# Agent attention with two feed-forward layers on one core: q blocks among k, two v blocks a step, combined weights inside the last q steps

## Chip, cores and metric

One core of a Trainium2 chip. The metric is the device time of one execution in microseconds (us); lower is better.

## What is computed

```python
scale = 1.0 / np.sqrt(q.shape[-1])
def sm(a, b):
    s = scale * (a @ b.transpose(0, 2, 1))
    s = s - s.max(-1, keepdims=True)
    e = np.exp(s)
    return e / (e.sum(-1, keepdims=True) + 1e-09)
agent_v = sm(agents, k) @ v          # 49 agents, k and v: 12480 x 128
x = sm(q, agents) @ agent_v          # q: 12480 x 128
h = x @ w_in                         # 128 x 2048
x = (h * (1.0 / (1.0 + np.exp(-h)))) @ w_out
h = x @ w2_in
out = (h * np.cos(h)) @ w2_out
```

q, k, v and agents are fp32. The four weight matrices come as 64-bit floats, 128 x 2048 or 2048 x 128.

## The kernel before

Precision is kept by splitting: a number is held as a high and a low part in the fp32r type, and a product is three matmuls (high x high, low x high, high x low). Each of the 16 weight pieces (512 columns of 64-bit words) is taken apart by `split_a` and `split_b`: an absolute value on ACT (L260), five DVE operations on the words (L264, L265, L269, L272, L275), a cast on ACT for the high part (L285), two POOL operations for the low part (L286, L287).

The 12480 rows of q, k and v are cut into 13 blocks (12 of 1024 rows and one of 192). The work goes through three stages.

1. **k pass.** For each k block, `T` turns the raw rows on PE (L323: eight 128 x 128 transposes into `h`) and ACT copies them to SBUF (`xT`, L327). `k_scores` multiplies by the agents (L357), ACT keeps the scores (`sT`, L360) and DVE takes a running maximum (`kmax`, L361). Ten weight pieces are split in the same steps.
2. **q steps.** Step i turns q block i, computes the scores of q block i-1 (`q_scores`, L337) and their exponentials (`q_exp`: maximum L117, subtraction L120, Exp L121), normalises block i-2 (`q_norm`: sum L128, + 1e-9 L130, reciprocal L132, product on POOL L133), splits block i-3 (`q_split`: L145 to L147, tile `pk`) and turns block i-4 in two halves (`p_out`: transposes L156 into the PSUM bank `y2`, copy to `pT` L161). The maximum over all k is made by `k_max_b` and `k_max_c` (result `mk`, L380). A list `at` says in which step a k block gets its exponential (`k_exp`, L383); its turn (`k_turn`, L394, copy `eT` L396) and its product with v (`av`, L408, summed in the bank `pav`) follow one and two steps later. In nearly all steps that is one k, v block.
3. **End of the attention.** `pav` is brought together (`halves`, L472, L475), normalised (`ag`, L479) and spread (`pn`, L481). The first product of layer 1 is not made with x: the agents' values are multiplied into `w_in` first, so that layer 1 takes the 49 probabilities `pT` and combined weights. This is `av_times_w` (L550 to L552, with the high and low parts `avh`, `avl` of the agents' values), `apart` (`hr` L557, four subtractions into `w3` L560) and `in_place` (L564, L565, L568 write `w2l`, `w2h`). It stands behind the attention, in the part whose order is written out by hand.

Then follow 25 blocks of up to 512 tokens through both layers. `L1_rest` (L590) and `L1_h` (L602) make h, `L1_act` the Silu (L610), `L1_y` (L634, L635, L638) the output; layer 2 follows five groups (`LAG`) behind. The in-place pair of the last quarter of the combined weights stands in group 1 of this loop.

What sets the order: up to the end of the attention the framework's scheduler orders the instructions of each engine by dependencies and by the order in the code; the splitting of weights has a lower priority (`LATER`). Every engine takes its instructions in order, and so does the SP queue, which issues all loads. The list `todo` sets the order of q, k and v loads: all k, then q and v in turn, with `NRAW` (7) buffers for q and k, `NV` (3) for v and 3 for weight pieces (`wraw`). From the combined weights on, the order is the one written in the code.

Of the kernel before, what the change touches and what calls it, by code (L numbers as in the profile page):

```python
# [22 lines left out]
NRAW = 7  # L23
NV = 3
# [4 lines left out]
LAG = 5  # L29
LINE = 32  # L30
# [3 lines left out]
def agent_attention_moe_moe_kernel(ctx, tc, q, k, v, agents, w_in, w_out, w2_in, w2_out, out):  # L34
# [79 lines left out]
    def q_exp(S, ps, between):  # L114
# [26 lines left out]
    def q_split(S):  # L141
        _, p, n = blocks[S]
        e = es.pop(S)
# [24 lines left out]
    def p_out_two(S):  # L168
        pp = bank2()
        for g in range(2):  # L170
            p_turn(S, g, pp[:, g, :])
        for g in range(2):
            p_keep(S, g, pp[:, g, :], nc.scalar.copy)

    with ExitStack() as att:
# [3 lines left out]
        eT_p = att.enter_context(tc.tile_pool(name="eT", bufs=2))  # L179
# [11 lines left out]

        ag = one_p.tile([NA, C], F32, name="ag")
# [678 lines left out]
```

## Time and profile before

| | |
|---|---|
| median of 3 runs | 1120.99 us (1120.79 to 1121.43) |
| profiled execution | 1122.09 us |
| its span | 1120.3 us |
| PE busy | 1085.3 us, 97% |
| DVE busy | 979.1 us, 87% |
| ACT busy | 923.9 us, 82% |
| POOL busy | 541.4 us, 48% |

The span is what the profiler recorded from the first to the last instruction of the profiled execution; its own time is 1.8 us longer. PE is one array with two rows in the views: PE for matmuls, PEld for weight loads. A busy share over the whole span says little here, since the long loop over both layers makes up most of it. The stages ahead of the loop are read by stretches and by timelines.

### The profile page before, as it was taken

What the parts mean: (1) busy time and instruction counts of PE and PEld (TensorE: products, weight loads), DVE (VectorE), ACT (ScalarE), POOL (GpSimd) and SP (SyncE); (2) the same over time, 40 slices, a digit from 0 to 9 for tenths busy, and PEclk for the clock granted to TensorE, in tenths of its full rate; (3) what the DMA queues carried; (4) which work ended last, traced back from release to release, by engine and by line L of the source; (5) the groups of instructions that cost most, each with busy time, mean ns of one, the idle gap of its engine ahead of it and who ended that gap; (6) DMA issues with size and microseconds to landing.
All of it is one profiled execution on the core that took longest, in us unless ns stands there. A gap on an engine that the chain in (4) does not pass through costs nothing.

```text
span 1120.3 us, 14139 instructions
## 1 busy us (share of the span) xinstructions
PE 1085.3 (97%) x5227; PEld 850.5 (76%) x5227; DVE 979.1 (87%) x1053; ACT 923.9 (82%) x1006; POOL 541.4 (48%) x278
## 2 busy tenths in 40 slices
PE   8878899999999999999999999999999999999997
PEld 4667666777777777777777777777777777788996
DVE  5898369999999999999999999999999999999997
ACT  6757588888888888888888888888888888888876
POOL 2578303444455544445554444555444455555455
PEclk9889889999999999999999999999999999999999
DMA  8655100000000000000000000000000000000000
GB/s 321 228 207 192 53 6 6 1 16 16 10 6 16 16 1 16 16 10 6 16 15 1 16 16 11 6 16 15 1 16 16 11 6 14 14 1 14 10 8 16
DMA packets 66221, 38.68 MB, mean 35 GB/s; under 512 B 52523, under 2 KB 57184, under 8 KB 66152
## 3 DMA queue, kind: packets, MB, share of 16 engines
q1 hardware_dynamic: 66152, 37.78, 11.3%
q8 instruction: 41, 0.67, 0.3%
q14 instruction: 28, 0.23, 0.1%
HBM read 27.58 MB, written 6.39 MB: 30 GB/s over the span
## 4 chain that ended last, share of the span: by engine, by line
PE 82%; ACT 2%; DVE 1%; issue 1%; POOL 1%; POOLq 0%; ACTq 0%; DVEq 0%
PE y L634 15%; PE y L638 15%; PE y L635 15%; PE h L602 9%; PE h L676 8%; PE h L678 8%; PE h L677 8%; PE h L590 4%; ACT g L610 1%; POOL g2l L735 1%; DVE g L717 1%; ACT n L690 0%; ACT g1h L617 0%; DVE n L700 0%; DVE g2h L726 0%
## 5 line engine op out<-in xcount | busy, mean ns | idle before, releaser
L735 POOL TENSOR_TENSOR g2l<-g,g2h 128x1024 fp32r<-128x1024 f32 (+2 forms) x200 | 465.5, 2349 | 512.6 <-DVE g1l L625 502.8
L700 DVE SCALAR_TENSOR_TENSOR n<-n,h 128x1024 f32<-128x1024 int32 (+3 forms) x202 | 239.1, 1185 | 65.2 <-ACT n L690 52.0
L690 ACT ACTIVATE n<-h,quarter 128x1024 int32<-128x1024 f32 (+3 forms) x202 | 219.8, 1089 | 89.3 <-PE h L678 89.3
L625 DVE TENSOR_TENSOR g1l<-g,g1h 128x1024 fp32r<-128x1024 f32 (+2 forms) x200 | 239.7, 1198 | 16.8 <-ACT g1h L617 9.6
L717 DVE TENSOR_TENSOR g<-n,h 128x1024 f32<-128x1024 f32 (+3 forms) x202 | 238.0, 1179 | 3.3 <-ACT n L709 0.2
L610 ACT ACTIVATE g<-h 128x1024 f32<-128x1024 f32 (+2 forms) x200 | 199.6, 998 | 36.4 <-PE h L602 36.3
L709 ACT ACTIVATE n<-n,halfpi 128x1024 f32<-128x1024 f32 (+3 forms) x202 | 225.6, 1119 | 0.8 <-DVE n L700 0.8
L617 ACT CAST g1h<-g 128x1024 fp32r<-128x1024 f32 (+2 forms) x200 | 204.8, 1024 | 3.3
L726 DVE CAST g2h<-g 128x1024 fp32r<-128x1024 f32 (+2 forms) x196 | 154.3, 788 | 7.5
L634 PE MATMUL y<-g1h,o1h 128*128 128x512 f32 (+2 forms) x400 | 156.7, 392 | 0.6 <-DVE x2l L663 0.5
L634 PE MATMUL y<-g2h,o2h 128*128 128x512 f32 (+2 forms) x400 | 154.5, 386 | 1.1 <-DVE o L757 0.9
L676 PE MATMUL h<-x2h,i2h 128*128 128x512 f32 (+2 forms) x400 | 154.1, 385 | 1.0 <-DVE g L717 1.0
L635 PE MATMUL y<-g2h,o2l 128*128 128x512 f32 (+2 forms) x400 | 154.4, 386 | 0.0
L635 PE MATMUL y<-g1h,o1l 128*128 128x512 f32 (+2 forms) x400 | 154.2, 386 | 0.0
L678 PE MATMUL h<-x2l,i2h 128*128 128x512 f32 (+2 forms) x400 | 153.7, 384 | 0.0
L677 PE MATMUL h<-x2h,i2l 128*128 128x512 f32 (+2 forms) x400 | 153.7, 384 | 0.0
L602 PE MATMUL h<-pT,w2h 128*128 128x512 f32 (+2 forms) x400 | 132.9, 414 | 0.0
L638 PE MATMUL y<-g2l,o2h 128*128 128x512 f32 (+2 forms) x400 | 122.2, 386 | 1.9 <-POOL g2l L735 1.9
L638 PE MATMUL y<-g1l,o1h 128*128 128x512 f32 (+2 forms) x400 | 121.6, 385 | 0.0
L634 PEld LDWEIGHTS y<-g1h,o1h 128*128 128x128 f32 x400 | 75.3, 188 | 22.0 <-DVE x2l L663 8.5
L602 PEld LDWEIGHTS h<-pT,w2h 128*128 128x128 f32 x400 | 67.6, 189 | 31.0 <-issue 24.0
L638 PEld LDWEIGHTS y<-g2l,o2h 128*128 128x128 f32 x400 | 74.8, 188 | 17.7 <-POOL g2l L735 3.1
(131 smaller groups left out, 1183.8 us busy)
## 6 DMA issues: line engine op xcount, KB each, us to landing
raw<-in_q_dram SPq DMA_DIRECT2D x12, 512.0 KB
vraw<-in_v_dram SPq DMA_DIRECT2D x12, 512.0 KB
raw<-in_k_dram SPq DMA_DIRECT2D x11, 512.0 KB
out_dram<-o SPq DMA_DIRECT2D x88, 64.0 KB
wraw<-in_moe_w_in_dram SPq DMA_DIRECT2D x8, 512.0 KB
wraw<-in_moe_w_out_dram SPq DMA_DIRECT2D x8, 512.0 KB
x<-pT SPq DMA_DIRECT2D x88, 38.0 KB
raw<-in_k_dram SPq DMA_DIRECT2D x2, 256.0 KB
```

The lines of the kernel that those rows point to most:

```text
L602: nc.tensor.matmul(out=h1s[g, k][:, j, :toks(t)], lhsT=w2h[:, 128 * c:128 * c + 128], rhs=x, start=False, stop=True)
L625: i = v.tensor_tensor(out=gl, in0=f, in1=b32(gh), op=ALU.subtract)
L634: nc.tensor.matmul(out=y, lhsT=wh[:, c, :], rhs=gh[:, j, :], start=(c == 0), stop=False)
L635: nc.tensor.matmul(out=y, lhsT=wl[:, c, :], rhs=gh[:, j, :], start=False, stop=False)
L638: nc.tensor.matmul(out=y, lhsT=wh[:, c, :], rhs=gl[:, j, :], start=False, stop=(c == NCH - 1))
L676: nc.tensor.matmul(out=y, lhsT=i2h[:, c, :], rhs=xh, start=True, stop=False)
L677: nc.tensor.matmul(out=y, lhsT=i2l[:, c, :], rhs=xh, start=False, stop=False)
L678: nc.tensor.matmul(out=y, lhsT=i2h[:, c, :], rhs=xl, start=False, stop=True)
L700: v.scalar_tensor_tensor(out=b32(n)[:, p], in0=n[:, p], scalar=-2.0 * PI, in1=h2s[g, k][:, p], op0=ALU.mult, op1=ALU.add)
L709: sc.activation(out=r[:, p], in_=r[:, p], func=AF.Sin, bias=halfpi)
L717: v.tensor_tensor(out=f[:, p], in0=r[:, p], in1=h[:, p], op=ALU.mult)
L735: i = (v if (g, k) == (NG - 1, 1) else gp).tensor_tensor(out=gl[:, p], in0=f[:, p], in1=b32(gh)[:, p], op=ALU.subtract)
```

## The change

- **Order.** Three q steps (`EARLY_Q`) run inside the k pass, behind k blocks 4, 7 and 10, without weight splitting; six pieces (`EARLY_W`) are split there instead of ten. Behind the k pass a loop goes on with the q steps and takes two k, v blocks in each (`at[S] = 1 + S // 2`): exponentials in step b, turn and product in step b + 1.
- **Loads.** `todo` follows that order. Buffers: raw 5 instead of 7, v 4 instead of 3, `eT` 3 instead of 2.
- **Combined weights.** `avh`, `avl` and `combine` now stand inside the two q steps behind the last v product, in the part that the scheduler orders, two pairs of column blocks through the bank `h2`; the last q steps follow. Nothing of it is left in the loop of layer 1.
- **The 1e-9** of a q block's sum is a 50th column of three fixed tiles `three_e`, so the addition L130 goes.
- The small Silu that loads its table has no other input than `ones`; the scheduler now puts it at the start of ACT.

```text
lines of the changed kernel: turn L325, xT L329, q scores L339, k scores L359,
sT L362, k exponential L385, k turn L396, eT L398, av L410, pn L489,
combined weights L497 to L499, hr L504, w3 L507, in place L513 to L515,
L1_rest L612, L1_h L624, Silu L632
```

```diff
-NRAW = 7
-NV = 3
+NRAW = 5
+NV = 4
 NWARM = 9
 LATER = 150
 WIDE = 512
 LAST = (416, 416, 384)
 LAG = 5
+EARLY_Q = (4, 7, 10)
+EARLY_W = (2, 4, 6, 8, 10, 12)
...
-        e = e_p.tile([128, 8, NA], F32, tag="e", name="e")[:p, :n]
+        es[S] = three_e[S % 3][:p, :n]
+        e = es[S][:, :, 0:NA]
...
         z = e_p.tile([128, 8], F32, tag="z", name="z")[:p, :n]
-        nc.vector.tensor_reduce(out=z, in_=e, op=ALU.add, axis=AX.X)
-        run(between, 1)
-        nc.vector.tensor_scalar(out=z, in0=z, scalar1=1e-9, scalar2=None, op0=ALU.add)
+        nc.vector.tensor_reduce(out=z, in_=es[S], op=ALU.add, axis=AX.X)
...
-        eT_p = att.enter_context(tc.tile_pool(name="eT", bufs=2))
+        eT_p = att.enter_context(tc.tile_pool(name="eT", bufs=3))
         xT_p = att.enter_context(tc.tile_pool(name="xT", bufs=2))
...
+        three_e = [one_p.tile([128, 8, NA + 1], F32, name=f"e{j}") for j in range(3)]
...
-        todo = [(k, "k", S) for S in range(NS)]
-        for S in range(NS + 2):
-            todo += [(q, "q", S)] if S < NS else []
-            todo += [(v, "v", S - 2)] if S >= 2 else []
+        at = [1 + S // 2 for S in range(NS)]
+        todo, t = [], 0
+        for S in range(NS):
+            todo.append((k, "k", S))
+            if S in EARLY_Q:
+                todo.append((q, "q", t))
+                t += 1
+        for b in range(NS):
+            todo += [(q, "q", t + b)] if t + b < NS else []
+            todo += [(v, "v", S) for S in range(NS) if at[S] == b]
...
+        def q_step(t):
+
+            if t < NS:
+                T("q", t)
+            if 4 <= t < NS + 4:
+                p_out(t - 4, 0)
+            split_b()
+            load_piece()
+            work = split_a() if t >= len(EARLY_Q) else []
+            if 2 <= t < NS + 2:
+                q_norm(t - 2, work)
+            if 3 <= t < NS + 3:
+                q_split(t - 3)
+            run(work, 1)
+            if 1 <= t < NS + 1:
+                q_scores(t - 1)
+                q_exp(t - 1, pss.pop(("q", t - 1)), work)
+            run(work, 6)
+
+        def q_step_end(t):
+            if 4 <= t < NS + 4 and groups(t - 4) == 2:
+                p_out(t - 4, 1)
+
         for _ in range(2):
             load_piece()
-        work = []
+        t = 0
         for i in range(NS + 1):
-            T(*(("k", i) if i < NS else ("q", 0)))
+            if i < NS:
+                T("k", i)
             if i >= 1:
                 k_scores(i - 1)
-            if i >= 2 and i % 6 != 5:
+            if i in EARLY_Q:
+                q_step(t)
+                t += 1
+            if i in EARLY_W:
                 split_b()
-                work = split_a()
-                run(work, 6)
+                run(split_a(), 6)
                 load_piece()
 
-        at = [2, 3, 4, 5, 6, 6, 7, 8, 9, 10, 10, 11, 12]
-        for i in range(1, NS + 2):
-            if i < NS:
-                T("q", i)
-            if i == 2:
+        k_max_b()
+        early = t
+        while t < early + 3 or raws or todo:
+            b = t - early
+            for S in range(NS):
+                if at[S] == b - 1:
+                    k_turn(S)
+            q_step(t)
+            if b == 0:
                 k_max_c()
-            if i >= 4:
-                p_out(i - 4, 0)
             for S in range(NS):
-                if at[S] == i:
+                if at[S] == b:
                     k_exp(S)
-                if at[S] == i - 1:
-                    k_turn(S)
-            split_b()
-            load_piece()
-            work = split_a()
-            if i >= 2:
-                q_norm(i - 2, work)
-            if i >= 3:
-                q_split(i - 3)
-            run(work, 1)
-            if i <= NS:
-                q_scores(i - 1)
-                q_exp(i - 1, pss.pop(("q", i - 1)), work)
-            run(work, 6)
-            if i == 1:
-                k_max_b()
-            for S in range(NS):
-                if at[S] == i - 2:
+                if at[S] == b - 1:
                     av(S)
-            if i >= 4:
-                p_out(i - 4, 1)
-        while half_split or loaded or to_load:
-            split_b()
-            load_piece()
-            run(split_a(), 6)
-
-        halves = xT_p.tile([128, 2, 512], F32, tag="xT", name="halves")[:, 0, :C + 1]
+            q_step_end(t)
+            t += 1
+
...
-        p_out_two(NS - 2)
-        end = banky("y2")
-        p_turn(NS - 1, 0, end)
+        avh, avl = (eT_p.tile([128, 512], F32R, tag="eT", name=nm)[:, :256] for nm in ("avh", "avl"))
+        nc.vector.tensor_copy(out=avh, in_=pn)
+        nc.vector.tensor_tensor(out=avl, in0=pn, in1=b32(avh), op=ALU.subtract)
+
...
+        def combine(j, cast):
+            pair = bank2()
+            for x in range(2):
+                av_times_w(pair[:, x, :], j + x, True)
+            apart(pair, j, cast)
+            pair = bank2()
+            for x in range(2):
+                av_times_w(pair[:, x, :], j + x, False)
+            in_place(pair.rearrange("p x d -> p (x d)"), slice(512 * j, 512 * j + 1024))
+
+        for j, cast in ((0, nc.vector.tensor_copy), (2, nc.scalar.copy)):
+            q_step(t)
+            combine(j, cast)
+            q_step_end(t)
+            t += 1
+        while t < NS + 4:
+            q_step(t)
+            q_step_end(t)
+            t += 1
+        assert not (half_split or loaded or to_load or es)
...
-        b01, a01, b23 = pair_bank(), pair_bank(), pair_bank()
-        a2, a3 = banky("y1"), banky("y2")
...
-            if g == 1:
-                in_place(a3, q3)
-                in_place_low(a3, q3)
```

How the instructions move. In the names, `h` with a number is a PSUM tile of scores or turned rows, `y` with a number a bank of turned probabilities, `raw` and `vraw` loaded rows.

PE in a middle step, from one q score block to the next. Before:

```order
L408 MATMUL y_173<-vraw,eT 49x128 x5
L156 MATMUL y_867<-ident,pk 128x128 x4
L408 MATMUL y_173<-vraw,eT 49x128
L394 MATMUL h_891<-ident,sT 128x128 x4
L323 MATMUL h_794<-ident,raw 128x128 x8
L156 MATMUL y_884<-ident,pk 128x128 x4
L408 MATMUL y_173<-vraw,eT 49x128 x7
L156 MATMUL y_947<-ident,pk 128x128 x4
L337 MATMUL h_919<-agT,xT 128x98 x8
```

After:

```order
L156 MATMUL y_880<-ident,pk 128x128 x4
L396 MATMUL h_886<-ident,sT 128x128 x4
L396 MATMUL h_893<-ident,sT 128x128 x4
L156 MATMUL y_911<-ident,pk 128x128 x4
L339 MATMUL h_937<-agT,xT 128x98 x5
L325 MATMUL h_900<-ident,raw 128x128 x8
L339 MATMUL h_937<-agT,xT 128x98 x3
L410 MATMUL y_175<-vraw,eT 49x128 x16
```

One v block's eight products stood in pieces between the other work; now sixteen products of two blocks follow each other, and two k turns stand between two halves of probabilities.

ACT at the end of the attention, up to the first Silu of layer 1. Before:

```order
L161 CAST pT<-y_1441 128x512
L145 CAST pk<-e 96x2x49
L161 CAST pT<-h_1464 128x512 x2
L161 CAST pT<-y_1476 128x192
L545 ACT_TABLE_LOAD
L545 ACTIVATE silu<-ones 128x1
L564 ACTIVATE w2l<-h,from_67 32x1024
L565 CAST w2h<-h 96x1024
L557 CAST hr<-h 128x1024
L564 ACTIVATE w2l<-y_1541,from_67 32x512
L565 CAST w2h<-y_1541 96x512
L610 ACTIVATE g_1593<-h 128x1024
```

After:

```order
L513 ACTIVATE w2l<-h_1430,from_67 32x1024
L514 CAST w2h<-h_1430 96x1024
L161 CAST pT<-y_1446 128x512
L504 CAST hr<-h_1461 128x1024
L513 ACTIVATE w2l<-h_1474,from_67 32x1024
L514 CAST w2h<-h_1474 96x1024
L161 CAST pT<-y_1484 128x512
L145 CAST pk<-e_121 96x2x49
L161 CAST pT<-y_1490 128x512
L161 CAST pT<-y_1501 128x512
L632 ACT_TABLE_LOAD
L632 ACTIVATE g_1573<-h 128x1024
```

The in-place writes move ahead of the last probability copies, and the table load now stands directly in front of the first Silu instead of ahead of the combined weights.

PE in the k pass, from the turn of k block 5. Before:

```order
L323 MATMUL h_272<-ident,raw 128x128 x8
L357 MATMUL h_285<-xT,agk 64x512 x2
L323 MATMUL h_304<-ident,raw 128x128 x8
L357 MATMUL h_317<-xT,agk 64x512 x2
L323 MATMUL h_323<-ident,raw 128x128 x8
L357 MATMUL h_336<-xT,agk 64x512 x2
L323 MATMUL h_355<-ident,raw 128x128 x8
```

After, from the turn of q block 0:

```order
L325 MATMUL h_278<-ident,raw 128x128 x8
L325 MATMUL h_307<-ident,raw 128x128 x8
L359 MATMUL h_320<-xT,agk 64x512 x2
L325 MATMUL h_326<-ident,raw 128x128 x8
L359 MATMUL h_339<-xT,agk 64x512 x2
L325 MATMUL h_358<-ident,raw 128x128 x8
L359 MATMUL h_371<-xT,agk 64x512 x2
L325 MATMUL h_377<-ident,raw 128x128 x8
L339 MATMUL h_395<-agT,xT 128x98 x8
L325 MATMUL h_408<-ident,raw 128x128 x8
```

Turns of q blocks 0 and 1 and the scores of q block 0 stand among the k blocks; q block 0's scores come behind the turn of q block 1, eight rows after its own turn.

## Rows read from the trace of the kernel before

**Rows 1.** Busy time by stretches (us; PE, PEld, DVE, ACT, POOL, clock, DMA, GB/s).
```profile
0.00:37.00 37.00, 31.51 (x174) 16.22 (x175) 24.02 (x54) 25.46 (x37) 8.80 (x13) 1.00 0.81 301
37.00:121.00 84.00, 68.51 (x544) 59.83 (x543) 70.66 (x118) 56.87 (x110) 61.78 (x57) 0.88 0.57 197
121.00:138.00 17.00, 13.16 (x90) 9.20 (x88) 5.91 (x18) 6.25 (x14) 5.29 (x10) 0.74 0.06 23
```

**Rows 2.** Timeline, 20 to 46 us (start, us, engine, line, operation).
```profile
24.73 1.08 PE L357 MATMUL h<-xT,agk 128*64 128x512 f32 x4 [1.67 <-ACT xT L327]
...
43.76 0.16 DVE L380 TENSOR_SCALAR mk<-y 128x1 f32<-128x1 f32 x1 [0.88 <-PE y L379]
```

**Rows 3.** Timeline of PE, 45 to 61 us.
```profile
46.92 3.70 PE L337 MATMUL h<-agT,xT 128*128 128x98 f32 x16 [0.84 <-DVE z L130]
...
51.36 1.09 PE L323 MATMUL h<-ident,raw 128*128 128x128 f32 x8
52.29 0.60 PE L156 MATMUL y<-ident,pk 128*128 128x128 f32 x4
52.82 0.86 PE L408 MATMUL y<-vraw,eT 128*49 128x128 f32 x12
...
58.86 2.03 PE L337 MATMUL h<-agT,xT 128*128 128x98 f32 x16
```

**Rows 4.** Groups of DVE by line, 0 to 148 us (busy us, mean ns).
```profile
L269 DVE SCALAR_TENSOR_TENSOR a<-wraw,a 128x512 uint32<-128x512 uint32 x16 | 17.8, 1110 | 0.2
L265 DVE TENSOR_SCALAR a<-m 128x512 uint32<-128x512 uint32 x16 | 14.5, 909 | 0.2
L275 DVE SCALAR_TENSOR_TENSOR r<-wraw,m 128x512 f32<-128x512 uint32 x16 | 14.0, 874 | 0.2
L272 DVE TENSOR_SCALAR m<-a 128x512 uint32<-128x512 uint32 x16 | 10.2, 640 | 0.1
L264 DVE TENSOR_SCALAR m<-m 128x512 f32<-128x512 f32 x16 | 9.3, 581 | 1.8 <-ACT m L260 1.8
...
L117 DVE TENSOR_REDUCE m<-h 128x8 f32<-128x392 f32 (+1 forms) x13 | 6.9, 534 | 9.5 <-PE h L337 9.5
```

**Rows 5.** Line 130 alone (duration ns: min, median, max).
```profile
L130 DVE TENSOR_SCALAR z<-z x13: 157/330/1246, 46.7 to 125.4; 128x8 f32<-128x8 f32 x12, 96x2 f32<-96x2 f32 x1
```

**Rows 6.** Timeline of all engines, 128 to 149 us.
```profile
128.92 0.51 PE L408 MATMUL y<-vraw,eT 96*49 96x128 f32 x2 [3.00 <-DMA vraw<-in_v_dram]
...
136.25 0.43 DVE L542 TENSOR_TENSOR avl<-h,avh 128x256 fp32r<-128x256 f32 x1
...
138.18 0.80 PE L550 MATMUL h<-w2h,avh 128*128 128x512 f32 x1 [0.84 <-ACT pT L161]
...
138.37 1.28 ACT L545 ACT_TABLE_LOAD   x1
...
139.66 0.20 ACT L545 ACTIVATE silu<-ones 128x1 f32<-128x1 f32 x1
...
141.20 1.22 DVE L557 CAST hr<-h 128x1024 fp32r<-128x1024 f32 x1 [4.52 <-PE h L552]
...
142.46 1.72 DVE L560 TENSOR_TENSOR w<-h,hr 32x256 fp32r<-32x256 f32 x4
...
143.37 1.11 ACT L564 ACTIVATE w2l<-h,from 32x1024 fp32r<-32x1024 f32 x1 [3.51 <-issue]
...
144.50 1.01 ACT L565 CAST w2h<-h 96x1024 fp32r<-96x1024 f32 x1
...
145.54 1.23 DVE L568 TENSOR_TENSOR w2h<-h,w2l 32x1024 fp32r<-32x1024 f32 x1 [1.36 <-ACT w2h L565]
...
148.03 1.02 ACT L610 ACTIVATE g<-h 128x1024 f32<-128x1024 f32 x1 [0.31 <-PE h L602]
```

**Rows 7.** Timeline of ACT, 154 to 158 us: two Silus of layer 1.
```profile
154.04 1.02 ACT L610 ACTIVATE g<-h 128x1024 f32<-128x1024 f32 x1
...
157.35 1.02 ACT L610 ACTIVATE g<-h 128x1024 f32<-128x1024 f32 x1
```

More of the change, by code (lines that the diff above doesn't have):

```diff
@@ L142, in q_split @@
         _, p, n = blocks[S]
-        e = es.pop(S)
+        e = es.pop(S)[:, :, 0:NA]
         pk = pk_p.tile([128, 8, 128], F32R, tag="pk", name="pk")[:p, :n]
@@ L166, in p_out @@
         p_keep(S, g, pp, copy)
[L168 to L173, printed above, removed]
     with ExitStack() as att:
@@ L291, in agent_attention_moe_moe_kernel @@
         nc.vector.memset(ones, 1.0)
+        for e in three_e:
+            nc.gpsimd.memset(e[:, :, NA:NA + 1], 1e-9)
         for a in (0, NA, 2 * NA):
@@ L466, in agent_attention_moe_moe_kernel @@
+            q_step_end(t)
+            t += 1
+        halves = one_p.tile([128, C + 1], F32, name="halves")
         nc.gpsimd.memset(halves, 0.0)
-        q_split(NS - 1)
+        assert not todo and not raws
         avn = ag
@@ L481, in agent_attention_moe_moe_kernel, with av_times_w, apart, in_place @@
         nc.tensor.matmul(out=pn, lhsT=avn, rhs=eye3, start=True, stop=True)
-        p_out_two(NS - 2)
-        end = banky("y2")
-        p_turn(NS - 1, 0, end)
+        avh, avl = (eT_p.tile([128, 512], F32R, tag="eT", name=nm)[:, :256] for nm in ("avh", "avl"))
+        nc.vector.tensor_copy(out=avh, in_=pn)
+        nc.vector.tensor_tensor(out=avl, in0=pn, in1=b32(avh), op=ALU.subtract)
+        def av_times_w(y, j, apart):
+            cs, a = slice(512 * j, 512 * j + 512), slice(128, 256) if apart else slice(0, 128)
+            nc.tensor.matmul(out=y, lhsT=avh[:, a], rhs=w2h[:, cs], start=True, stop=False)
+            nc.tensor.matmul(out=y, lhsT=avh[:, a], rhs=w2l[:, cs], start=False, stop=False)
+            nc.tensor.matmul(out=y, lhsT=avl[:, a], rhs=w2h[:, cs], start=False, stop=True)
+        def apart(pw, j, cast):
+            hr = v_p.tile([128, 2, 512], F32R, tag="v", name="hr")
+            cast(out=hr, in_=pw)
+            for i in range(4):
+                rows, d = slice(32 * i, 32 * i + 32), slice(128 * i, 128 * i + 128)
+                nc.vector.tensor_tensor(
+                    out=w3[rows, j:j + 2, :], in0=pw[rows, :, d], in1=b32(hr)[rows, :, d], op=ALU.subtract
+                )
+        def in_place(y, cs):
+            nc.scalar.activation(out=w2l[96:128, cs], in_=y[96:128], func=AF.Identity, scale=from98[96:128])
+            nc.scalar.copy(out=w2h[0:96, cs], in_=y[0:96])
+            nc.vector.tensor_tensor(out=w2h[96:128, cs], in0=y[96:128], in1=b32(w2l)[96:128, cs], op=ALU.subtract)
+        def combine(j, cast):
[17 more added lines that the diff above has]
+        assert not (half_split or loaded or to_load or es)
     pre.close()
@@ L538, in agent_attention_moe_moe_kernel @@
         steady.enter_context(tc.manual_schedule())
-        avh, avl = (g1l_p.tile([128, 2, WIDE], F32R, tag="g1l", name=nm)[:, 0, :256] for nm in ("avh", "avl"))
-        v.tensor_copy(out=avh, in_=pn)
-        v.tensor_tensor(out=avl, in0=pn, in1=b32(avh), op=ALU.subtract)
-        p_keep(NS - 1, 0, end, sc.copy)
         sc.activation(out=silu, in_=ones[:, 0:1], func=AF.Silu)
-        def av_times_w(y, j, apart):
-            cs, a = slice(512 * j, 512 * j + 512), slice(128, 256) if apart else slice(0, 128)
-            nc.tensor.matmul(out=y, lhsT=avh[:, a], rhs=w2h[:, cs], start=True, stop=False)
-            nc.tensor.matmul(out=y, lhsT=avh[:, a], rhs=w2l[:, cs], start=False, stop=False)
-            nc.tensor.matmul(out=y, lhsT=avl[:, a], rhs=w2h[:, cs], start=False, stop=True)
-        def apart(pw, j, cast):
-            hr = g1h_p.tile([128, 2, 512], F32R, tag="g1h", name="hr")
-            cast(out=hr, in_=pw)
-            for i in range(4):
-                rows, d = slice(32 * i, 32 * i + 32), slice(128 * i, 128 * i + 128)
-                v.tensor_tensor(out=w3[rows, j:j + 2, :], in0=pw[rows, :, d], in1=b32(hr)[rows, :, d], op=ALU.subtract)
-        def in_place(y, cs):
-            sc.activation(out=w2l[96:128, cs], in_=y[96:128], func=AF.Identity, scale=from98[96:128])
-            sc.copy(out=w2h[0:96, cs], in_=y[0:96])
-        def in_place_low(y, cs):
-            v.tensor_tensor(out=w2h[96:128, cs], in0=y[96:128], in1=b32(w2l)[96:128, cs], op=ALU.subtract)
         def L1_rest_in(t):
```

19 lines of the change are left out of this document (1 added, 18 removed).

## Prediction

> **What bounds the kernel now.** I read the busy time by stretches first [rows 1]. It shows three stretches ahead of the long steady loop: a k pass up to 37 us, a middle with q blocks, k exponentials and v products up to 121 us, and an end. In the middle VectorE (DVE) is busy 70.7 of 84 us, PE 68.5, GpSimd (POOL) 61.8, ACT 56.9: DVE sets the pace, the others have room. In the end, from 121 to 138 us, DVE and ACT work only 5.9 and 6.3 of 17 us. The timeline of that end [rows 6] says why: PE waits 3.00 us for the last v block, then one thing follows another (the second part of the agent values, `avl`, is ready at 136.68 us, the first combined-weight matmul starts at 138.18, the first Silu of layer 1 at 148.03). From there on the code of both layers is the same, so I place the change by when the first Silu starts.
>
> **The change, in the order of time.**
>
> *The k pass.* Three q blocks are now turned among the k blocks. In the new PE order two more turns and almost two more q score blocks stand ahead of the step that makes the maximum known (`mk`, now at 43.76 us [rows 2]). By the rows of PE [rows 3]: from the start of a turn of a raw block to the next work are 0.93 us (51.36 to 52.29), from a group of four transposes to the next 0.53 (52.29 to 52.82); each row's own time is 0.07 to 0.16 us more, the overlap. A score block takes 2.03 us, about 1.96 without it. That is 2 x 0.93 + 2 x 1.96 = 5.8 us. There is also a new wait: `xT` has two buffers, and a q block's copy holds one until its scores, several k steps later. The k blocks share the other, so a copy must wait for the scores before it; a stall of this kind cost 1.67 us once before [rows 2]. For some six k steps I put 0.25 us each, 1.5 us; zero if ACT keeps up, 5 us if an ACT cast that waits for DVE gets between. Queued behind each such copy on ACT are the next `sT` copy and the weight casts. So `mk` comes at 43.8 + 5.8 + 1.5 = 51 us (48 to 55). That is 7 us lost, paid for by three q blocks that are then done.
>
> *Loads.* On the SP queue q loads now stand among k loads, raw buffers fall from 7 to 5, and weight loads wait for the split of the piece three before; behind each stand k or q loads. The k pass asks for 13 k, 5 q and some 8 weight blocks of 0.52 MB, about 13 MB in 46 us, 290 GB/s; a middle step asks for four blocks, 2.1 MB in 7.7 us, 270 GB/s. The first stretch moved 301 GB/s [rows 1]. I cost the queue at nothing; its cover is one step of lead, and without it a step would grow by a wait like the 3.00 us [rows 6].
>
> *From `mk` to the scores of q4:* in the new order three half-blocks of probabilities, two turns of exponentials, one raw turn, one score block and the rest of another. 5 x 0.53 + 0.93 + 1.96 + 0.25 = 5.8 us, and 1 us for the first exponential: 58 us.
>
> *Six steps, q5 to q10, two v blocks in each.* PE: 0.93 + 1.96, two v products of 1.07 (twelve of their sixteen matmuls took 0.86 [rows 3], 0.80 without the overlap), two pairs of transposes 4 x 0.53: 7.15 us. The sixth has the short v block: 6.4. Sum 42.2 us. DVE: seven weight pieces fall into these six steps, each 1.11 + 0.91 + 0.87 + 0.64 + 0.58 = 4.11 us, and a q block costs three ops like the 0.53 one and a reciprocal, about 1.8 us [rows 4]: 7 x 4.11 + 6 x 1.8 = 39.6 us. So PE becomes the bound with DVE close behind. If the busiest engine reached only DVE's share in the middle now, 84% [rows 1], the six steps would take 50 us; without any waiting 42. I take 46, since PE has fewer engines ahead of it in its order than DVE had: scores of q10 end at 104 us. The dropped addition of 1e-9 (6.6 us of DVE by 13 x 0.51, but the shortest took 0.157 [rows 5]) I cost at nothing, because PE's 42 us hide it; if that cover goes it gives at most the 6.6.
>
> *From there to `avl`:* the last v product, a small turn, two transposes and the scores of q11 on PE, about 4 us; then on DVE, in the new order, q11's maximum and subtraction, the last piece, the normalisation and `avl`, 6.3 us by the rows above. `avl` at 114.4 us, against 136.68.
>
> *Combined weights.* They move ahead of the last probability blocks, in pairs, and do not get shorter. After `avl`: about 2 us of matmuls, 0.7 us of the last piece in front on DVE, then 1.22 (`hr`), 1.72 (four parts of `w3`), 0.4 for q12's small ops, 1.23 (low part), 1.6 us of matmuls for the second pair, whose bank was held, 1.11 and 1.01 (in place), 1.23 [rows 6]. That is 12.2 us. Layer 1's first matmul waits for that last op in the new order; with its own four matmuls and one group of transposes in front it comes to 14.2. ACT meanwhile has three probability copies and a load of the Silu table of 1.28 us in front of the first Silu, which ends at about 15. So 15 us after `avl`, where now it takes 11.35: first Silu at 129.4 us instead of 148.03, a gain of 18.6.
>
> *Layer 1.* The in-place pair of the last quarter stood between two Silus: 154.04 to 157.35, 3.31 us instead of 2.01 [rows 7]. It goes, 1.3 us; one small probability copy, 0.3 us, comes in.
>
> **Sum.** -18.6 - 1.3 + 0.3 = -19.6 us from the profiled execution's 1122.09: 1102.5. That execution stands 1.1 us above the median of the runs, so I forecast **1101 us**. Low: `mk` at 48, the six steps at 42.2, the end 1 us shorter, 1093. High: `mk` at 55, the steps at 50, the matmuls of the end at a clock nearer the lower level, 0.74 having been granted from 121 to 138 us [rows 1] (2.5 us more, an estimate), 1112. A measurement of this kernel can tell about 0.2%, 2.2 us, from no change.
>
> **One rule weighed.** The load of the Silu table took 1.28 us and the next activation started 0.01 us after it [rows 6]; I count 1.28. The Trainium skill ("ScalarE: Activation LUTs", "What ACT_TABLE_LOAD costs") says that a switch to another set costs a drain of about 1380 ns besides. It speaks against this change, and by it, for two switches, the time would be 1104; this case's trace does not show the drain.
>
> **Rivals.**
>
> *DVE and POOL block each other (1112 us).* The tiny addition took between 0.157 and 1.246 us [rows 5], so DVE waits at times for something other than its inputs. If each of the five ops of a piece waited another half microsecond, about half of the longest wait seen, 7 x 5 x 0.5 = 17.5 us would meet the 6.4 us that DVE has free in 46: +11 us. For it: both engines are dense in the middle [rows 1]. Against: POOL's work per piece does not change. The Trainium skill ("SBUF — State Buffer", "Who interferes with whom") says that a DVE op with two SBUF inputs and a POOL op that reads SBUF exclude each other for a whole instruction; by that rule the wait of a removed op only moves to the next, and the dropped addition gives 2 us of DVE, not 6.6.
>
> *Slower: PE's steps at the lower clock (1135 us).* The granted clock was 0.88 in the middle, and one score block took 3.70 us instead of 2.03 [rows 1, 3]. A step of 7.15 us would take some 5.7 us more at that ratio. Four of the six steps eat the gain; all six give 1101 + 34 = 1135. For it: the middle already fell below the full 2.4 GHz. Against: in that stretch PE sat idle 15 of 84 us, in the new steps hardly, and in the k pass, with the same transposes back to back, the clock was 1.00 [rows 1].
>
> *The table switches cost double (1104 us).* In the new ACT order an Exp load stands in the k pass and a Silu load in front of layer 1, where now the one load of the end falls into a wait. If each held ACT for a second 1.28 us, that adds 2.6 us. Against it: the 0.01 us above.
>
> *The order does not deliver (1121 us).* What is certain to be lost is 7 us at `mk` and 3.7 us after `avl`. The part between, 92.9 us now, must shrink from there; if the six steps took 10.9 us each instead of 7.7, nothing would be left. No row speaks for so long a step.
>
> **Chances.** Forecast with its own bounds 0.76; blocked DVE 0.10; table switches 0.06; nothing gained 0.03; slower 0.05. Faster by over 0.2%: 0.92, the first three; same 0.03; slower 0.05. The range 1093 to 1112 holds the first three cases but for their edges, a little over 8 in 10.
>
> **What would show it.** `mk` near 51 us; scores of q4 to q10 every 7.5 us with PE over 90% busy at full clock; `avl` near 114 and the first Silu near 129 us; a table load right in front of it; Silus 2.0 us apart from the first on; the long loop unchanged. Steps over 9 us, a granted clock under 0.8 between 58 and 104 us, or PE waiting for a v or weight load would make the prediction wrong.

## The result and the profile after

The changed kernel takes 1108.96 us (4 runs, 1107.95 to 1110.07) against 1120.89 us: ratio 0.9894, 95% interval 0.9877 to 0.9911. That is 11.9 us faster, inside the range of 1093 to 1112, but 8 us short of the 1101 forecast. The profiled execution took 1109.03 us, its span 1107.3 (before: 1122.09 and 1120.3).

The forecast was a sum of milestones, so the same milestones show where the 8 us are. "Ready" is the end of the operation:

| | before | forecast | measured | forecast of the step | measured |
|---|---|---|---|---|---|
| `mk` starts | 43.76 | 51 | 54.89 | | |
| q4 scores end | | 58 | 61.6 | 7 | 6.7 |
| q10 scores end | | 104 | 108.6 | 46 | 47.0 |
| `avl` ready | 136.68 | 114.4 | 119.15 | 10.4 | 10.5 |
| first Silu starts | 148.03 | 129.4 | 134.26 | 15 | 15.1 |
| end of the span, against before | | -19.6 | -13.0 | -1.0 behind the first Silu | +0.8 |

So 4.9 us are lost by the first Silu, 3.9 of them ahead of `mk` (0.5 of these at the first running maximum already, which starts at 11.05 us against 10.51), and 1.8 behind it. The rest is how the profiled execution stands to the median: 1.1 us above it before, as the forecast subtracted, nothing after.

Busy time of the changed kernel by stretches, columns as in [rows 1]:

```profile
37.00:55.00 18.00, 13.19 (x94) 9.49 (x95) 16.02 (x29) 12.84 (x21) 11.71 (x10) 1.00 0.74 266
55.00:61.50 6.50, 6.16 (x52) 5.53 (x51) 6.23 (x14) 6.18 (x14) 4.70 (x5) 1.00 0.67 241
61.50:88.50 27.00, 26.48 (x293) 24.82 (x294) 20.14 (x34) 26.71 (x57) 19.46 (x21) 1.00 0.79 274
88.50:104.15 15.65, 10.10 (x118) 9.00 (x114) 15.58 (x23) 8.94 (x20) 11.59 (x10) 0.96 0.56 182
104.15:119.00 14.85, 13.21 (x71) 11.50 (x72) 13.00 (x25) 7.79 (x16) 11.46 (x12) 0.70 0.03 12
119.00:134.00 15.00, 10.91 (x48) 7.54 (x46) 8.79 (x17) 10.10 (x14) 5.87 (x8) 0.87 0.03 11
```

The six steps are two regimes. From 61.5 to 88.5 us PE is busy 26.5 of 27 us at full clock: four steps in 26.7 us, 6.7 each, as the theory of PE as the bound has it (7.15). From 88.5 on DVE is full, 15.58 of 15.65 us, PE works two thirds of the time, and the steps of q9 and q10 take 8.2 and 12.1 us. The total of 47.0 is near the forecast of 46 because the first four were faster and the last two slower, which is luck.

What happens there: a timeline of PE, 98 to 106 us, then of ACT in the same time.

```profile
98.96 1.04 PE L325 MATMUL h<-ident,raw 128*128 128x128 f32 x8
104.15 1.09 PE L156 MATMUL y<-ident,pk 128*128 128x128 f32 x4 [4.16 <-ACT pT L161]
```

```profile
97.26 1.00 ACT L329 COPY xT<-h 128x1024 f32<-128x1024 f32 x1
101.92 0.68 ACT L260 ACTIVATE m<-wraw 128x512 f32<-128x512 f32 x1 [3.66 <-POOL o2l L287]
103.00 0.53 ACT L124 ACTIVATE e<-e 128x392 f32<-128x392 f32 x1
103.43 0.57 ACT L161 CAST pT<-y 128x512 fp32r<-128x512 f32 x1
```

The row of PE names ACT's copy of probabilities, which holds the bank `y2`. ACT had been waiting 3.66 us, since the absolute value of the next piece needs the tile `m`, which POOL still reads for the piece two before; the copy stands behind it in ACT's order. After this gap of 4.16 us PE's clock is granted at 0.70 on average up to 119 us: four turns take 1.09 us where they took 0.66 at 98.35, q10's scores 3.57 where q4's took 1.93.

In the k pass a piece stands on DVE between the running maximum and `mk` (DVE timeline, 50 to 55 us):

```profile
50.45 1.07 DVE L265 TENSOR_SCALAR a<-m 128x512 uint32<-128x512 uint32 x1
51.44 0.15 DVE L369 TENSOR_REDUCE m<-kmax 128x1 f32<-128x13 f32 x1
51.56 1.64 DVE L269 SCALAR_TENSOR_TENSOR a<-wraw,a 128x512 uint32<-128x512 uint32 x1
53.12 0.27 DVE L373 COPY mrow<-y 1x128 f32<-1x128 f32 x1
53.32 0.98 DVE L272 TENSOR_SCALAR m<-a 128x512 uint32<-128x512 uint32 x1
54.22 0.27 DVE L374 TENSOR_TENSOR mrow<-mrow,y 1x128 f32<-1x128 f32 x1
...
54.89 0.13 DVE L382 TENSOR_SCALAR mk<-y 128x1 f32<-128x1 f32 x1
```

The change does not lose its time there. From the maximum over all k blocks (L369) to `mk` are 3.45 us here, and 6.60 in the kernel before, where a piece stood there too:

```profile
37.16 0.15 DVE L367 TENSOR_REDUCE m<-kmax 128x1 f32<-128x13 f32 x1
```

The loss lies ahead of the maximum, which comes 14.28 us later (51.44 against 37.16). PE waits there for the copies to `xT`, five times, where before it waited once for 1.67 us [rows 2] (waits of PE, 10 to 52 us: us in total, times, longest):

```profile
PE h L359 <- ACT xT L329: 7.3, 5, 2.5
```

The longest of these waits, followed back over ACT to DVE:

```profile
22.94 1.08 PE L359 MATMUL h<-xT,agk 128*64 128x512 f32 x4 [2.49 <-ACT xT L329]
```

```profile
21.36 0.62 ACT L285 CAST w2h<-a 128x512 fp32r<-128x512 f32 x1 [2.44 <-DVE a L269]
```

```profile
19.68 1.64 DVE L269 SCALAR_TENSOR_TENSOR a<-wraw,a 128x512 uint32<-128x512 uint32 x1
```

A cast on ACT waits for a slow DVE operation of a piece, and the copy to `xT` stands behind the cast. After this wait the clock is granted at 0.54 from 26 to 28 us, and a k score block takes 1.98 us instead of 1.08.

The tail behind `avl`, all engines, which answers to [rows 6]:

```profile
118.73 0.42 DVE L493 TENSOR_TENSOR avl<-h,avh 128x256 fp32r<-128x256 f32 x1
...
123.88 0.47 PE L497 MATMUL h<-w2h,avh 128*128 128x512 f32 x1 [1.63 <-DVE w L507]
...
129.21 1.23 DVE L515 TENSOR_TENSOR w2h<-h,w2l 32x1024 fp32r<-32x1024 f32 x1 [0.89 <-ACT w2h L514]
...
130.49 0.79 PE L612 MATMUL h<-x,w 19*128 19x512 f32 x2
...
132.97 1.28 ACT L632 ACT_TABLE_LOAD   x1
...
134.26 1.02 ACT L632 ACTIVATE g<-h 128x1024 f32<-128x1024 f32 x1
```

Every wait that the forecast named is there: the second pair waits for `w3`, layer 1 for the last low part, the table load stands right in front of the first Silu. And behind it (ACT, 138 to 144 us, against [rows 7]):

```profile
138.35 1.02 ACT L632 ACTIVATE g<-h 128x1024 f32<-128x1024 f32 x1
...
140.70 1.03 ACT L632 ACTIVATE g<-h 128x1024 f32<-128x1024 f32 x1 [0.26 <-PE h L624]
...
143.19 1.03 ACT L632 ACTIVATE g<-h 128x1024 f32<-128x1024 f32 x1 [0.39 <-PE h L624]
```

The Silus now wait for PE. From the first to the tenth are 19.35 us before (148.03 to 167.38) and 19.53 after (134.26 to 153.79), though the in-place pair is gone.

### The profile page after: what moved, and what is told of

It reads as the page before. It is cut to its first block, busy times and chain, and to the rows that moved or that the text cites. A ratio compares the mean times of both kernels' runs of the same rounds, so it can differ in the third digit from the quotient of the medians.

```text
span 1107.3 us, 14127 instructions
## 1 busy us (share of the span) xinstructions
PE 1074.7 (97%) x5227; PEld 844.5 (76%) x5227; DVE 972.4 (88%) x1039; ACT 924.5 (83%) x1005; POOL 540.6 (49%) x281
## 4 chain that ended last, share of the span: by engine, by line
PE 89%; DVE 5%; ACT 2%; issue 1%; DMA 1%; POOL 1%; SPq 0%; POOLq 0%; DVEq 0%; ACTq 0%
PE y L656 16%; PE y L657 16%; PE y L660 16%; PE h L624 10%; PE h L698 8%; PE h L700 8%; PE h L699 8%; PE h L612 4%; PE h L339 1%; DMA wraw<-in_moe_w_in_dram 1%; DVE a L269 1%; PE y L156 1%; PE h L325 1%; DVE r L275 1%; POOL g2l L757 0%
```

## The experiments

My theory after this profile: in the middle DVE and POOL, not PE, set the time wherever weight pieces are dense, since they hold each other up; that delays `mk`, then q9 and q10. The rivals were the two `xT` buffers, ACT's order, and parts of the change that bring nothing. Differences to the changed kernel are taken from the two ratios, times 1121 us; with intervals of about 0.0017 on either side, less than some 3 us is not told apart. Milestones come from one profiled execution each, and these do not start alike: the first weight piece begins on DVE at 14.16 us in the changed kernel and between 12.95 and 15.43 in the runs below. "From the first piece" means that this is taken off.

### Parts of the change undone

**One k, v block a step.**

```diff
-        at = [1 + S // 2 for S in range(NS)]
+        at = [1 + S for S in range(NS)]
...
-        for b in range(NS):
+        for b in range(NS + 2):
```

> One k, v block a step instead of two, all else as in the changed kernel. Theory (the gain is that the v products end together with the q steps): mk stays at 55 us, q10 is done by about 105 us, but three or four k, v blocks are left behind q12 and avl comes near 130 us instead of 119.2; the tail behind avl shrinks from 15 to about 11 us since no q block is left in it. First Silu 141 to 144 us, time 1116 to 1119 us. Rival (the pieces on DVE set the steps whatever stands on PE): first Silu within 3 us of 134.3, time 1107 to 1112 us.

Ratio 0.9923 (0.9907 to 0.9940), 1113.15 us: some 3 us slower, its interval just touching that of the changed kernel. The place was right, the size not: q12's scores end at 103.9 us, the v products only at 116.3, `avl` starts at 122.81 and the first Silu at 137.59. The blocks left over cost less than forecast, and the tail did not shrink (14.8 us): DVE and ACT need it for the combined weights whether q blocks stand in it or not.

**No early q blocks.**

```diff
-EARLY_Q = (4, 7, 10)
+EARLY_Q = ()
...
-        while t < early + 3 or raws or todo:
+        while t < early + 9:
...
```

> No q block among the k blocks; the two k, v blocks a step, the combined weights inside the last q steps and the six early weight pieces stay. Theory (three q blocks fill waits of the k pass): mk falls back to about 44 us, a gain of 11, but three more q steps of about 6 us stand ahead of layer 1: first Silu near 141 us, time 1114 to 1117 us. Rival (what the early q blocks cost in the k pass equals what they save): time 1107 to 1111 us.

Ratio 0.9946 (0.9927 to 0.9965), 1115.16 us, 5.8 us slower. In the profiled execution (its longest, 1118.36 us) `mk` falls back to 45.08 and the first Silu comes at 141.61. The theory holds: three q blocks in the k pass cost 10 us at `mk` and save more, since without them the q steps stand behind `avl` (115.48) and the first Silu comes 26 us after it.

**Combined weights behind the last q step.**

```diff
         for j, cast in ((0, nc.vector.tensor_copy), (2, nc.scalar.copy)):
             q_step(t)
-            combine(j, cast)
             q_step_end(t)
             t += 1
...
+        for j, cast in ((0, nc.vector.tensor_copy), (2, nc.scalar.copy)):
+            combine(j, cast)
```

> The combined weights behind the last q step, as before, all else as in the changed kernel. Theory (inside the q steps they share the time of the last four): the last probability block is out near 128 us, then 11 us as before (11.35 from avl to the first Silu): first Silu near 138 us, time 1111 to 1114 us. Rival (from avl on the chain hr, w3, in place on DVE and ACT sets the time wherever the last q steps stand): 134 us, time 1107 to 1111 us.

Ratio 0.9891 (0.9876 to 0.9906): the rival. `avl` starts 2.2 us earlier, at 116.52, and the first Silu at 134.08. This part of the change brought nothing that these runs can tell; whichever work goes first, the other is behind it.

**The addition of 1e-9 back.**

```diff
-        nc.vector.tensor_reduce(out=z, in_=es[S], op=ALU.add, axis=AX.X)
+        nc.vector.tensor_reduce(out=z, in_=e, op=ALU.add, axis=AX.X)
         run(between, 1)
+        nc.vector.tensor_scalar(out=z, in0=z, scalar1=1e-9, scalar2=None, op0=ALU.add)
```

> The separate addition of 1e-9 is back on DVE, 13 instructions (the sum takes the 49 columns alone). Theory (hidden while PE sets the steps, paid where DVE does): 13 times 0.33 us, the median of before, is 4.3 us of DVE; of these only the some five between 88 and 119 us are on the path: +1.5 us, time 1109 to 1112 us. Rival 1 (DVE sets the whole middle): +4 to +6.6 us, 1113 to 1116 us. Rival 2 (hidden altogether): 1109 us.

Ratio 0.9934 (0.9919 to 0.9949), 1114.25 us, 4.5 us slower: the first rival, and the step that I had cost at nothing. The group of DVE in that run (busy us, mean ns):

```profile
L132 DVE TENSOR_SCALAR z<-z 128x8 f32<-128x8 f32 (+1 forms) x13 | 5.9, 456 | 0.1
```

13 operations that take 157 ns at their shortest hold DVE for 5.9 us, the longest of them for 1.23. `mk` comes 2.6 us later (3.2 from the first piece), `avl` 3.7, the first Silu 5.6. But this is not simply DVE's time. The five operations of a piece got shorter, 3.83 us together instead of 4.11, the first of them most (this run, then the changed kernel):

```profile
L265 DVE TENSOR_SCALAR m<-m 128x512 f32<-128x512 f32 x16 | 8.7, 547 | 2.4 <-ACT m L261 2.4
```

```profile
L264 DVE TENSOR_SCALAR m<-m 128x512 f32<-128x512 f32 x16 | 10.9, 680 | 1.5 <-ACT m L260 1.5
```

Over sixteen pieces that is 4.5 us less, so DVE is busy only 1.4 us longer in all. The order of DVE's operations in the k pass changes with the edit as well. By which path the 4.5 us reach the end is not shown.

### The suspects

**The early q blocks' `xT` in tiles of their own.**

```diff
-            xt = xT_p.tile([128, 2, 512], F32, tag="xT", name="xT")[:, :, :h * p]
+            early_q = key == "q" and S < len(EARLY_Q)
+            xt = (home(2 + S, "xTq", F32).rearrange("p (g d) -> p g d", g=2) if early_q else xT_p.tile([128, 2, 512], F32, tag="xT", name="xT"))[:, :, :h * p]
```

> The turned rows of the three early q blocks get tiles of their own, so that the k blocks keep both xT buffers. Theory (a q block that holds one of two buffers for several k steps makes the k blocks follow one another): the k scores end 3 to 5 us before 49.6, mk comes at 50 to 52 us instead of 54.9, time 1104 to 1106 us. Rival (in the k pass ACT and DVE wait for each other over weight casts, table load and slow pieces, whatever the buffers): mk within 1 us of 54.9, time 1107 to 1111 us.

Ratio 0.9927 (0.9906 to 0.9949), 1112.37 us: not faster. Yet the theory's first half holds in part: the k scores end at 46.3 instead of 49.6 us, `mk` starts at 52.42, 2.5 us earlier, of which 1.6 remain from the first piece. PE then waits for the running maximum on DVE instead, 4.4 us in three places. The gain is lost later, at a wait of PE that the changed kernel does not have:

```profile
80.85 1.09 PE L325 MATMUL h<-ident,raw 128*128 128x128 f32 x8 [1.95 <-DMA raw<-in_q_dram]
```

A q block arrives late, and `avl` starts at 119.98. In the changed kernel the loads have no such wait in the middle.

**`m` free before POOL.**

```diff
-                nc.gpsimd.tensor_tensor(out=m, in0=a.bitcast(F32), in1=b32(hi), op=ALU.subtract)
-                nc.gpsimd.tensor_tensor(out=lo, in0=r, in1=m, op=ALU.add)
+                nc.gpsimd.tensor_tensor(out=a.bitcast(F32), in0=a.bitcast(F32), in1=b32(hi), op=ALU.subtract)
+                nc.gpsimd.tensor_tensor(out=lo, in0=r, in1=a.bitcast(F32), op=ALU.add)
```

> POOL's first operation on a piece writes its result over a instead of m, so that m is free as soon as DVE has done with it and ACT's next absolute value need not wait for POOL. Theory (ACT held for 8.6 us by that wait between 88 and 110 us makes the long steps of q9 and q10, 8.2 and 12.1 us): these steps take 7 to 8 us, avl comes 4 to 6 us earlier than 118.7, time 1103 to 1105 us. Rival (DVE is full there, 19.9 of 20.1 us, and ACT only waits because DVE and POOL are late): the wait moves to DVE's write of a, avl within 1.5 us of 118.7, time 1107 to 1111 us.

Ratio 0.9920 (0.9900 to 0.9941), 1111.64 us: not faster. The waits of 88 to 122 us (who waits for whom: us in total, times, longest) show where ACT's wait went; the profiled execution is again the longest, 1114.06 us:

```profile
PE y L156 <- ACT pT L161: 6.4, 3, 3.8
...
ACT o2h L285 <- DVE a L269: 5.2, 3, 3.2
```

ACT now waits for DVE, 5.2 us in three places, and PE behind it as before (6.4 us, 5.5 in the changed kernel). Freeing `m` moved ACT's wait and did not shorten PE's.

**A fill in place of POOL's two operations.** The low parts of the weights are left out.

```diff
-                nc.gpsimd.tensor_tensor(out=m, in0=a.bitcast(F32), in1=b32(hi), op=ALU.subtract)
-                nc.gpsimd.tensor_tensor(out=lo, in0=r, in1=m, op=ALU.add)
+                nc.gpsimd.memset(b32(lo), 0.0)
```

> POOL's two operations on a weight piece, which read two tiles in SBUF, are replaced by one fill with zeros: the low parts of the weights are left out of the computation. Theory (DVE operations on SBUF tiles wait while POOL reads SBUF): L265, L272 and L264 fall to 0.43 us each in nearly all pieces, L269 and L275 to 0.69, a piece from 4.11 to 2.7 us; mk comes 2 to 4 us earlier, the steps of q9 and q10 take 7 us, time 1098 to 1102 us. Rival (something else stretches them, such as loads that write SBUF): the five operations keep a mean of over 3.8 us a piece, time 1106 to 1110 us.

Ratio 0.9779 (0.9762 to 0.9795), 1096.07 us: 12.9 us faster than the changed kernel, by far the largest effect of all. `mk` starts at 48.84 (6.1 us earlier, 4.8 from the first piece), `avl` at 105.09, the first Silu at 123.02. The fills wait for nothing, and POOL has done all sixteen before DVE begins its first piece at 12.95 us; the last four:

```profile
7.23 1.93 POOL L286 MEMSET o2l<- 128x512 f32 x4
```

So the run shows DVE with nothing of a piece left on POOL, and not beside a POOL that only writes. One line's durations (min/median/max in ns), L269 and L265, in the changed kernel:

```profile
L269 DVE SCALAR_TENSOR_TENSOR a<-wraw,a x16: 681/756/1644, 15.1 to 116.1; 128x512 uint32<-128x512 uint32 x16
...
L265 DVE TENSOR_SCALAR a<-m x16: 411/814/1486, 14.6 to 115.3; 128x512 uint32<-128x512 uint32 x16
```

and without POOL's two operations:

```profile
L269 DVE SCALAR_TENSOR_TENSOR a<-wraw,a x16: 681/693/757, 13.9 to 103.7; 128x512 uint32<-128x512 uint32 x16
...
L265 DVE TENSOR_SCALAR a<-m x16: 414/420/949, 13.4 to 102.5; 128x512 uint32<-128x512 uint32 x16
```

L269 hardly waits any more. L265 still does at times, by up to 0.53 us, beside POOL's product for a q block, and so does L275, by up to 0.8 us (DVE and POOL of this run):

```profile
95.95 0.95 DVE L265 TENSOR_SCALAR a<-m 128x512 uint32<-128x512 uint32 x1
```

```profile
95.59 1.02 POOL L133 TENSOR_TENSOR e<-e,z 128x392 f32<-128x392 f32 x1
```

A piece costs DVE 3.01 us instead of 4.11 (by the means of its five lines). The edit also takes from POOL the 2.6 us a piece that the two operations need themselves; how much of the 12.9 us is that, and how much DVE's waiting, the run does not tell apart. How such a wait looks, in the changed kernel, DVE and then POOL, 86 to 90 us:

```profile
86.16 1.21 DVE L275 SCALAR_TENSOR_TENSOR r<-wraw,m 128x512 f32<-128x512 uint32 x1
87.38 1.08 DVE L264 TENSOR_SCALAR m<-m 128x512 f32<-128x512 f32 x1
88.50 1.38 DVE L265 TENSOR_SCALAR a<-m 128x512 uint32<-128x512 uint32 x1
```

```profile
85.92 0.90 POOL L133 TENSOR_TENSOR e<-e,z 128x392 f32<-128x392 f32 x1 [1.09 <-ACT eT L398]
86.84 1.34 POOL L147 TENSOR_TENSOR pk<-e,pk 128x392 fp32r<-128x392 f32 x1
88.14 1.45 POOL L286 TENSOR_TENSOR m<-a,i2h 128x512 f32<-128x512 f32 x1
```

Each DVE operation ends 0.3 to 0.6 us after the POOL operation that runs beside it (87.37, 88.46, 89.88 against 86.82, 88.18, 89.59). It stands in DVE's row all the while, and what is left of it then is 0.12 to 0.13 us less than the shortest time of its line (0.67, 0.41, 0.41). The Trainium skill ("SBUF — State Buffer", "Who interferes with whom") says that a DVE operation with two SBUF inputs and a POOL operation that reads SBUF block each other for a whole instruction, and that `tensor_scalar` in its fast modes contends with POOL too. The trace agrees beside POOL operations that read: L275 has two inputs, L264 and L265 are `tensor_scalar`, and all three end only after them. No run here shows either beside a POOL operation that only writes. That the lock is the reason is the Trainium skill's; the runs show that the waits go when POOL's operations go.

**One piece fewer in the k pass.** This was to take away the piece between the maximum and `mk`.

```diff
-EARLY_W = (2, 4, 6, 8, 10, 12)
+EARLY_W = (2, 4, 6, 8, 10)
```

> Five weight pieces in the k pass instead of six: the one behind k block 12, whose operations stand on DVE between the running maximum and mk, goes to a later step. Theory (mk is held by these, 1.07 + 1.64 + 0.98 us between kmax and mk): mk 2 to 3 us earlier, but one piece more for DVE where it is full between 88 and 119 us, so that avl comes within 1 us of 118.7 and the time is 1107 to 1111 us. Rival (DVE has room in the four steps set by PE): the gain at mk stays, avl near 116 us, time 1105 to 1107 us.

Ratio 0.9898 (0.9884 to 0.9913), 1108.96 us: no difference. But the edit did not take that piece away. DVE's order is the same up to 68 us, with the same operations behind the maximum:

```profile
50.61 0.15 DVE L369 TENSOR_REDUCE m<-kmax 128x1 f32<-128x13 f32 x1
50.72 1.64 DVE L269 SCALAR_TENSOR_TENSOR a<-wraw,a 128x512 uint32<-128x512 uint32 x1
...
54.05 0.14 DVE L382 TENSOR_SCALAR mk<-y 128x1 f32<-128x1 f32 x1
```

`mk` comes 0.8 us earlier because the first piece does (13.32 against 14.16 us). What moved is a later piece, from 69.3 to 72.9 us, so what the one at `mk` costs is not tested.

### Pieces moved out of the dense stretch

The last pieces belong to layer 2. A dependency on `avl` and a count keep the last two, or three, until then; three lines are added, so lines from 246 on stand 1 to 3 further down.

```diff
-            if not loaded:
+            if not loaded or (not behind and len(to_load) + len(loaded) <= 3):
...
-                nc.scalar.activation(out=m, in_=Hf, func=AF.Abs)
+                i = nc.scalar.activation(out=m, in_=Hf, func=AF.Abs)
+            for x in behind:
+                tc.add_manual_dep(i.ins, x.ins.name, AFTER, reason="behind avl")
...
-        nc.vector.tensor_tensor(out=avl, in0=pn, in1=b32(avh), op=ALU.subtract)
+        behind.append(nc.vector.tensor_tensor(out=avl, in0=pn, in1=b32(avh), op=ALU.subtract))
```

(With 2 in place of 3 for two pieces.)

> The last two weight pieces (needed only by layer 2) are split behind avl instead of between 88 and 119 us; nothing is left out. Theory (from 88 us on the pieces on DVE and POOL, which hold each other up, set the steps, while DVE is busy only 8.8 of 15 us behind avl): each piece taken out of there gives 4 to 5 us, avl comes at 109 to 112 us instead of 118.7; behind avl two pieces without POOL beside them take 2 times 2.65 us of DVE, half of it in gaps: first Silu 128 to 131 us instead of 134.3, time 1103 to 1106 us. Rival (the tail is one chain over ACT and DVE, so that a piece costs there what it saved): avl as above, first Silu 133 to 136 us, time 1107 to 1111 us.

Ratio 0.9895 (0.9878 to 0.9911), 1108.9 us: no gain. The profiled execution was its longest, 1113.89 us, so its milestones are not those of the median; in it PE waits 4.16 us at q10 again and the clock falls to 0.67 from 105 to 119 us. The third piece from the end still stands on DVE there, from 100.1 us on.

> The same with the last three pieces. Theory: avl at 105 to 108 us; the third piece comes behind the last combined weights, where DVE waits some 6 us for the first Silu's result in the changed kernel, so it costs nearly nothing there: first Silu 125 to 129 us, time 1100 to 1104 us. Rival (as for two pieces): first Silu 133 to 136 us, time 1107 to 1111 us.

Ratio 0.9855 (0.9839 to 0.9871), 1104.15 us: **faster than the changed kernel by 4.4 us**, the intervals apart, and the best version that computes everything. `avl` starts at 110.53, 8.2 us earlier; the first Silu at 130.03, since the tail grew from 15.5 to 19.5 us (start to start). By stretches:

```profile
88.00:105.00 17.00, 14.61 (x156) 13.02 (x155) 14.03 (x23) 10.16 (x21) 13.34 (x13) 1.00 0.53 171
105.00:119.00 14.00, 11.04 (x66) 8.66 (x65) 10.49 (x27) 9.69 (x19) 5.71 (x8) 1.00 0.06 23
119.00:134.00 15.00, 10.22 (x32) 6.04 (x31) 12.40 (x17) 10.90 (x16) 6.80 (x7) 0.62 0.01 1
```

```profile
101.07 0.63 PE L156 MATMUL y<-ident,pk 128*128 128x128 f32 x4 [1.20 <-ACT pT L161]
101.53 1.93 PE L342 MATMUL h<-agT,xT 128*128 128x98 f32 x16
```

DVE has room again, the gap at q10 is 1.20 us instead of 4.16, the clock stays full to 119 us, and the scores take 1.93 us instead of 3.57. The step of q10 takes 7.1 us instead of 12.1. The lower clock comes later, in the tail. The run takes the pieces off ACT and POOL as well, so it does not say which of the three engines had held PE.

**Three behind, with each of two earlier edits.** The tiles of their own for the early `xT`, and five pieces in the k pass.

> Three pieces behind avl, and the early q blocks' turned rows in tiles of their own. Theory (in e5 the 2.5 us won at mk were given back because the pieces of 88 to 119 us, not mk, set avl; with three of them gone the gain at mk gets through): mk at 52 us, avl at 107 to 109 us instead of 110.5, time 1101 to 1103 us. Rival (the pieces still set the steps): avl within 1 us of 110.5, time 1103 to 1106 us.

Ratio 0.9885 (0.9869 to 0.9901), 1107.84 us: 3.4 us worse than three behind alone, the intervals just touching. In its profiled execution (1110.03 us, its longest) `mk` starts at 55.41, only 0.6 us earlier from the first piece than in the changed kernel: it waits 1.12 us for its transpose, which stands on PE behind q scores and part of a turn, at a granted clock of 0.50 from 51 to 56 us (eight score matmuls take 1.87 us where sixteen took 1.93). PE also waits 1.67 us for a q block at 84.03, as in the run with these tiles alone. `avl` starts at 116.26. Neither theory nor rival.

> Three pieces behind avl, and five instead of six in the k pass. Theory (DVE has room again up to 105 us, 14.0 of 17 us busy in the last run with three pieces behind): mk 0.8 us earlier as in e8, the piece fits into a later step, avl at 109 to 111 us, time 1103 to 1105 us. Rival (a piece more in the steps from 88 us on brings back a long PE gap and the lower clock): avl at 113 to 117 us, time 1106 to 1110 us.

Ratio 0.9878 (0.9860 to 0.9896), 1106.91 us: the rival's time, though the intervals with three behind alone overlap. `mk` comes 0.5 us earlier, and the first piece just as much, since here too the piece at `mk` stays. Two PE gaps of 2.07 and 2.22 us come back at 92 and 95 us; `avl` starts at 112.32, between both expectations.

## Why the prediction was right, and where its sum was off

*The k pass (51 us, measured 54.89): mis-sized.* The term is the new wait for `xT`: 1.5 us in the sum, with 5 us for the case "if an ACT cast that waits for DVE gets between". That case came. PE waits 7.3 us for `xT` where it waited 1.67, 5.6 us more, and part of the pass runs at the lower clock. Tiles of their own for the early q blocks gave back 1.6 us of it from the first piece; without POOL's two operations `mk` comes 4.8 us earlier. So the k pass was costed by PE and ACT alone, while DVE's pieces hold up ACT in it. Between the maximum and `mk` the change lost nothing (3.45 us, before 6.60).

*"PE becomes the bound with DVE close behind": right for four steps of six, and the sum came near by luck.* I counted DVE's 39.6 us against 46 as a total. The pieces do not come evenly: DVE is busy 20 of 27 us in the first four steps and 15.6 of 15.7 in the next two. The mean of 4.11 us held the waits for POOL already [rows 4], but where POOL is dense they take more: the four pieces from 87 to 110 us 4.8, 5.6, 4.1 and 5.8 us. The prediction's own sign of being wrong, a step over 9 us, came true for q10 (12.1). The rival "DVE and POOL block each other" named this mechanism with a price of 11 us over the forecast; moving three pieces recovered 4.4 us, and taking POOL's two operations away, with the time that POOL needs for them, 12.9.

*"The dropped addition I cost at nothing, because PE's 42 us hide it": wrong.* With it back the kernel is 4.5 us slower, and some 3 of them are there at `mk`, ahead of the steps that were to hide it. What the prediction worked out beside the rule of the Trainium skill ("SBUF — State Buffer", "Who interferes with whom"), an estimate of 2 us of DVE since the wait of a removed operation moves to the next, is near the 1.4 us of the trace. So the 4.5 us are more than DVE's time, and their path stays open.

*"Combined weights": right, 15.1 against 15 us.* But the place brings nothing; the chain over DVE and ACT is the same behind the q steps.

*"It goes, 1.3 us": wrong.* The in-place pair in layer 1 was hidden: for two Silus PE needs about 4.3 us there, ACT 4.0. I read a gap on ACT without asking whether PE stood ahead.

*Full clock: right in the PE-bound steps, not around them.* The rival of the lower clock was placed in these steps, where the clock stayed at 1.00. It fell outside them, after waits of PE: in the k pass after 2.49 us (0.54 from 26 to 28 us), and at q10 after 4.16 us (0.70 up to 119 us).

*Table switches: no extra cost.* Both loads take 1.28 us; the first Exp (33.35) and the first Silu (134.26) each start 0.01 us after their load ends. The Trainium skill ("ScalarE: Activation LUTs", "What ACT_TABLE_LOAD costs") has a drain besides, which the prediction weighed; none is to be seen here.

By parts the 11.9 us are about 6 for the early q blocks, 4.5 for the addition and 3 for two v blocks a step, nothing for the place of the combined weights. These are differences with the rest in place, each with an order of its own, and need not add up. Not settled is how much of what tiles of their own won at `mk` was lost by the late load alone, since the order behind it changed too.

## What to carry to other kernels

Before a stage is costed by its busiest engine, look at the shortest and longest duration of one operation on one shape: DVE operations between 0.68 and 1.64 us had a wait for POOL inside the busy time (a piece took 1.1 us less without POOL's two operations), and DVE's busy share does not show it as such. A bound taken over several steps hides where the work lumps; moving what is not yet needed out of the lump (here three pieces that layer 2 uses) gave more than freeing buffers around it. A gap on one engine costs only if the engine behind it is not ahead of its own work. Before an edit's result is read, look in its trace whether it moved what it was to move, and take milestones from a common early event.

## What I had not expected

Thirteen operations on 8 elements a partition, put back, cost 4.5 us of 1109, though DVE was busy only 1.4 us longer. And an edit that ended the k scores 3.2 us earlier (2.4 from the first piece), with nothing added, made the kernel no faster: a load that had been in time was then late by 1.95 us.
